# Attention and an ELU feed-forward layer on one core: the ELU's sum left in PSUM, a planner that knows a shared port, and a fourth batch taken in front

## The chip, the core and the metric

The kernel runs on one core of one Trainium2 chip. A core has TensorE (PE in the profile: matrix products, from SBUF into PSUM), VectorE (DVE) and ScalarE (ACT), which read and write SBUF and PSUM, GpSimd (POOL), which this kernel uses on SBUF only, and SyncE (SP), which here issues the transfers. Each engine works through its own queue in order. What counts is the device time of one execution, in microseconds. The median of the runs before the change is 1211.21 us (1208.86 to 1212.19).

## The reference

Causal attention with a decay bias over 8 batches, 8 heads, 576 tokens and a head size of 64, then a feed-forward layer from 512 to 2048 and back over all 4608 tokens, with ELU between. In short:

```python
scores = scale * q @ k.T                          # scale = 1/8
cum    = cumsum(maximum(s, 0))                    # per head, over the tokens
scores = where(causal, -1e9, scores + minimum(-(cum[:, None] - cum[None, :]), 0))
attn   = exp(scores - max(scores)); attn /= sum(attn) + 1e-9
x      = (attn @ v), heads side by side           # (4608, 512)
h      = x @ w_in
g      = where(h > 0, h, exp(minimum(h, 0)) - 1)
out    = g @ w_out
```

The two weight matrices are given in 64 bits; the kernel makes 32-bit values of them itself.

## The kernel before, in words

**Precision.** A value is often split into a rounded high part and the difference that is left, so that a product in a fast format keeps its accuracy: three products (high by high, low by high, high by low) in the place of one. `rounded` (line 347) makes a high part on Pool, ACT or DVE, `rest` (line 359) a low part on DVE or Pool, `psum_copy` (line 367) copies out of PSUM on ACT or DVE.

**Attention.** The 576 queries of a head are cut into a first half block of 64 and four blocks of 128, numbered 0 to 3. A block's scores see only the keys up to its end. The first batches (`N_CUT` of them, so far three) are worked in two pieces. In front, a `Low` unit takes a pair of heads with the half block and blocks 0 and 1 at once (`CUT` is 2), in plain 32-bit products, with transposes on TensorE and little splitting. Later, two `Unit`s, one for each head, take blocks 2 and 3 ("late"). A batch that isn't cut has for each pair of heads one unit for the half blocks and two whole units for blocks 0 to 3. The units that are not `Low` split queries and keys, write their weights as two 16-bit parts (`halved`, line 867) and have them transposed by DMA. For each block, `softmax_block` issues the score products (line 838), an operation on DVE that adds the mask and takes the extreme (841), and the exponential on ACT (846). The result goes to DRAM in `x_dram`.

**Feed-forward part.** The tokens, in the order in which the pieces come, are cut into 12 chunks of 384. A chunk (`moe_chunk`, line 1111) loads its x, splits it into xh and xl, and goes through 16 hidden blocks. `hidden(f)` puts 12 products into a PSUM bank `h` (line 1131; two banks in turn). Then come the exponential on ACT into `g` in SBUF (1139), the minimum with 1 less 1 on DVE (1140), the sum with the positive part of h on DVE (1142), the high part `gh` and the low part `gl`. `project(f)` issues 9 products into three output banks (line 1155). PE's order there is by the planner, often one hidden block and one projection in turn.

**Weights.** 16 blocks of each of the two matrices come in as 64-bit words. DVE and one other engine turn each into 32-bit values (lines 485 to 504), then they are split. All are used by the first chunk.

**The planner.** Nothing is issued when it is written down. `Plan.op` records an operation with the ways to do it, each an engine with an estimated cost, and with what it reads and writes. `Plan.issue` then takes one operation after the other: that which can start earliest by its own clock, and of equal ones that with the smaller priority number. Of the ways, it takes the one with the smallest start plus cost, where the cost on DVE is multiplied by a bias. The result is a fixed order of the instructions on each engine; on the chip, an instruction starts when its queue comes to it and the semaphores of its operands are there. The planner's own times are not enforced.

Of the kernel before, what the change touches and what calls it, by code (L numbers as in the profile page):

```python
# [9 lines left out]
F32 = mybir.dt.float32  # L10
# [5 lines left out]
ALU = mybir.AluOpType  # L16
# [22 lines left out]
NATIVE, WHOLE = 0, 0  # L39


N_CUT, CUT = 3, 2
PRIO_LOW = 10
SP_COST = 430.0

# [26 lines left out]
class Plan:  # L72
# [15 lines left out]
    }  # L88
    HOP = 150.0

    BIAS = {"DVE": 2.0}

    def __init__(self, tc):
        self.tc, self.nc = tc, tc.nc
# [54 lines left out]
        )  # L149

    def issue(self):
        engines = sorted({w[0] for o in self.ops for w in o.ways})
        free = dict.fromkeys(engines, 0.0)
        taken = dict.fromkeys(self.tags, 0)
        slots, skipped = {}, {}
# [14 lines left out]
        while pending:  # L170
# [96 lines left out]
def dve_p(n):  # L267

    return 155 + 1.04 * n


def dve_1(n):

    return 165 + 0.7 * n


def dve_2(n):

    return 150 + 1.5 * n


def pool_1(n):
# [8 lines left out]
def kernel(  # L291
# [43 lines left out]
    op = plan.op  # L335
    act, dve, pool, pe_ = nc.scalar, nc.vector, nc.gpsimd, nc.tensor
# [10 lines left out]
    def rounded(prio, n, dst, src, reads, writes, sign=1.0, only=None):  # L347

        ways = [
            ("Pool", pool_1(n),  # L350
             lambda: pool.tensor_scalar(dst(), src(), sign, 1.0, ALU.mult, ALU.mult)),  # L351
            ("ACT", act_s(n),
             lambda: act.activation(dst(), src(), AF.Copy, scale=sign)),  # L353
            ("DVE", dve_1(n),
             lambda: dve.tensor_scalar(dst(), src(), sign, None, ALU.mult)),
        ]
        op(prio, [w for w in ways if only is None or w[0] in only], reads, writes)

    def rest(prio, n, dst, src, hi, reads, writes, only=None):

        ways = [
            ("DVE", dve_2(n), lambda: dve.tensor_tensor(dst(), src(), hi(), ALU.subtract)),  # L362
            ("Pool", pool_2(n), lambda: pool.tensor_tensor(dst(), src(), hi(), ALU.subtract)),  # L363
        ]
        op(prio, [w for w in ways if only is None or w[0] in only], reads, writes)
# [31 lines left out]
    def decay_sums():  # L397
# [14 lines left out]
        op(-9, [("DVE", 1900.0, sums)], [], [(aux, 0), (aux, 1)])  # L412
        op(-5, [("DVE", 1300.0, parts)], [(aux, 0)], [(aux, 1), (aux, 2)])
# [57 lines left out]
    def load_unit(f, kind, src, parts):  # L471
# [7 lines left out]
        if wide:  # L479
# [11 lines left out]
                ("DVE", 500.0, lambda: dve.tensor_scalar(  # L491
                    raw.v[:, :, 1].bitcast(F32), raw.v[:, :, 1].bitcast(F32),
                    2.0**-112, None, ALU.mult)),
            ], [], [(raw, 1)])
            op(prio, [("DVE", 500.0, lambda: dve.tensor_scalar(
                raw.v[:, :, 0], raw.v[:, :, 0], 2.0**-29, 7.0, ALU.mult, ALU.min))],
               [], [(raw, 0)])

            def gather():
                dve.scalar_tensor_tensor(  # L500
                    raw.v[:, :, 0], raw.v[:, :, 1], 0x80000000, raw.v[:, :, 0],
                    ALU.bitwise_and, ALU.bitwise_or,
                )
                dve.scalar_tensor_tensor(
                    raw.v[:, :, 0], raw.v[:, :, 1], 3, raw.v[:, :, 0],
                    ALU.logical_shift_left, ALU.bitwise_or,
                )
# [319 lines left out]
    def softmax_block(prio, tag, native, pt, w, mask, mv, reads, operands, inv, view=lambda v: v):  # L827
# [21 lines left out]
        if last:  # L849
            def inverse():  # L850
                dve.tensor_scalar(sm.v[:, :ns], sm.v[:, :ns], EPS, 1.0 / up, ALU.add, ALU.mult)  # L851
                dve.reciprocal(sm.v[:, :ns], sm.v[:, :ns])  # L852

            op(prio, [("DVE", 350.0, inverse)], [], [sm])

    def normalize(prio, pt, w, sm, col):
        r = slice(col, col + 1)
        op(prio, [
            ("Pool", 160 + 1.04 * w, lambda: pool.tensor_scalar(
                pt.v[:, :w], pt.v[:, :w], sm.v[:, r], 1.0, ALU.mult, ALU.mult)),  # L860
            ("DVE", 220 + 0.7 * w, lambda: dve.tensor_scalar(
                pt.v[:, :w], pt.v[:, :w], sm.v[:, r], None, ALU.mult)),
            ("ACT", 295 + w / 1.2, lambda: act.activation(
                pt.v[:, :w], pt.v[:, :w], AF.Copy, scale=sm.v[:, r])),
# [2 lines left out]
    def halved(u, i, pt, sm, col):  # L867
# [20 lines left out]
        for part, n in ((whole, k * P), (rest, HB))[: 1 + (i == u.last)]:  # L888
# [1 line left out]
            op(prio, [  # L890
                ("Pool", 160 + 1.04 * n, lambda part=part: pool.tensor_scalar(  # L891
                    part(t16, 0), own(part), sm.v[:, r], 1.0, ALU.mult, ALU.mult)),
                ("DVE", 220 + 0.7 * n, lambda part=part: dve.tensor_scalar(
                    part(t16, 0), own(part), sm.v[:, r], None, ALU.mult)),
                ("ACT", 295 + n / 1.2, lambda part=part: act.activation(  # L895
                    part(t16, 0), own(part), AF.Copy, scale=sm.v[:, r])),
            ], [sm, (pt, "data"), (pt, "pad")], [(t16, high)])
            op(prio, [
                ("DVE", dve_2(n), lambda part=part: dve.scalar_tensor_tensor(  # L899
                    part(t16, 1), own(part), sm.v[:, r], part(t16, 0), ALU.mult, ALU.subtract)),  # L900
                ("Pool", pool_1(n) + pool_2(n), lambda part=part: scaled_rest(part)),
            ], [sm, (pt, "pad"), (t16, high)], [(t16, low), (pt, "data")])
# [208 lines left out]
    def moe_chunk(ch, rows, xc, after):  # L1111
# [11 lines left out]
        parts = {}  # L1123

        def hidden(f):
            hp = plan.buf(ps, [P, TMAX], F32, f"h_{ch}_{f}", tag="h", bufs=N_H)
            for c in range(NCB):
# [12 lines left out]
            op(side, [("DVE", dve_1(TC), lambda: dve.tensor_scalar(  # L1140
                g.v[:, :TC], g.v[:, :TC], 1.0, -1.0, ALU.min, ALU.add))], [], [g])
            op(side, [("DVE", dve_p(TC), lambda: dve.scalar_tensor_tensor(  # L1142
                g.v[:, :TC], hp.v[:, :TC], 0.0, g.v[:, :TC], ALU.max, ALU.add))], [hp], [g])
# [134 lines left out]
```

## Time and profile before

| | |
|---|---|
| median of the runs | 1211.21 us (1208.86 to 1212.19) |
| the profiled execution, its own time | 1205.16 us |
| its span, first to last instruction | 1203.4 us |
| mean granted clock of TensorE | 0.991 |
| busy PE / DVE / ACT / POOL | 1117.1 / 859.7 / 608.9 / 819.5 us |

PEld is the weight loads of TensorE, which overlap its products. A line such as L1142 is a line of the kernel; where a helper records an operation the line is the helper's, and the tile tells which operation it is (`gl<-g,gh` on L363 is the low part of the ELU's result, made on Pool). The granted clock is TensorE's, as a share of full speed. "A <- B" in a list of waits means that A stood idle until B was done.

### The profile page before, as it was taken

What the parts mean: (1) busy time and instruction counts of PE and PEld (TensorE: products, weight loads), DVE (VectorE), ACT (ScalarE), POOL (GpSimd) and SP (SyncE); (2) the same over time, 40 slices, a digit from 0 to 9 for tenths busy, and PEclk for the clock granted to TensorE, in tenths of its full rate; (3) what the DMA queues carried; (4) which work ended last, traced back from release to release, by engine and by line L of the source; (5) the groups of instructions that cost most, each with busy time, mean ns of one, the idle gap of its engine ahead of it and who ended that gap; (6) DMA issues with size and microseconds to landing.
All of it is one profiled execution on the core that took longest, in us unless ns stands there. A gap on an engine that the chain in (4) does not pass through costs nothing. (4 is left out here: it accounts for less than half of the span.)

```text
span 1203.4 us, 19946 instructions
## 1 busy us (share of the span) xinstructions
PE 1117.1 (93%) x5992; PEld 950.5 (79%) x5992; DVE 859.7 (71%) x1903; ACT 608.9 (51%) x1500; POOL 819.5 (68%) x996
## 2 busy tenths in 40 slices
PE   5788887999999999999999999999999999999998
PEld 4577766778787778878878888878877887899996
DVE  6879999899877778768787777777787777422221
ACT  4676445554555554655555555445554554332322
POOL 6787888787877656867787777777776776332322
PEclk9899899999999999999999999999999999999999
DMA  7766566867676476566576565575665565210000
GB/s 197 205 160 201 156 153 150 194 146 150 162 155 129 103 167 125 123 157 128 127 170 139 122 165 128 130 172 122 128 149 129 123 140 128 60 53 1 27 1 27
DMA packets 342316, 156.55 MB, mean 130 GB/s; under 512 B 267560, under 2 KB 321088, under 8 KB 342208
## 3 DMA queue, kind: packets, MB, share of 16 engines
q1 hardware_dynamic: 342208, 155.27, 55.6%
q8 instruction: 48, 0.79, 0.3%
q14 instruction: 60, 0.49, 0.1%
HBM read 79.66 MB, written 19.32 MB: 82 GB/s over the span
## 5 line engine op out<-in xcount | busy, mean ns | idle before, releaser
L1131 PE MATMUL h<-xh,wi 128*128 128x384 f32 x1536 | 446.6, 341 | 9.7 <-DVE g L1142 9.6
L1155 PE MATMUL o<-wo,gh 128*128 128x512 f32 x1152 | 363.8, 397 | 2.2 <-DVE mn L841 1.5
L1131 PEld LDWEIGHTS h<-xh,wi 128*128 128x128 f32 x1536 | 284.4, 189 | 20.4 <-DVE g L1142 11.7
L363 POOL TENSOR_TENSOR gl<-g,gh 128x384 fp32r<-128x384 f32 x157 | 169.7, 1081 | 158.2 <-ACT gh L353 134.5
L1131 PE MATMUL h<-xl,wi 128*128 128x384 f32 x768 | 260.2, 339 | 3.9 <-DVE xl L362 1.8
L1155 PE MATMUL o<-wo,gl 128*128 128x512 f32 x576 | 229.8, 399 | 6.1 <-POOL gl L363 3.9
L1155 PEld LDWEIGHTS o<-wo,gh 128*128 128x128 f32 x1152 | 207.9, 189 | 30.7 <-DVE mn L841 2.3
L1140 DVE TENSOR_SCALAR g<-g 128x384 f32<-128x384 f32 x192 | 102.5, 534 | 168.5 <-ACT g L1139 167.3
L846 ACT ACTIVATE p<-p,mn 128x192 f32<-128x192 f32 (+1 forms) x232 | 144.9, 625 | 90.7 <-DVE mn L841 87.7
L1139 ACT ACTIVATE g<-h 128x384 f32<-128x384 f32 x192 | 93.8, 489 | 170.8 <-PE h L1131 119.0
L899 DVE SCALAR_TENSOR_TENSOR p<-p,sm,p 128x512 f16<-128x512 f32 (+3 forms) x179 | 167.2, 957 | 14.3 <-POOL p L891 12.1
L1131 PEld LDWEIGHTS h<-xl,wi 128*128 128x128 f32 x768 | 145.2, 189 | 13.1 <-POOL xl L363 4.2
L1155 PEld LDWEIGHTS o<-wo,gl 128*128 128x128 f32 x576 | 108.3, 188 | 38.0 <-POOL gl L363 9.0
L353 ACT ACTIVATE gh<-g 128x384 fp32r<-128x384 f32 x149 | 77.7, 521 | 119.6 <-DVE g L1142 119.2
L841 DVE CUSTOM_DVE_ANT_0 p<-sc,maskw 128x192 f32<-128x192 f32 (+1 forms) x232 | 110.1, 483 | 33.8 <-PE sc L838 28.8
L969 PE MATMUL av<-T,vs 128*128 128x256 f16 (+5 forms) x896 | 119.0, 285 | 5.1 <-DMA T<-p 2.7
L969 PEld LDWEIGHTS <-vs 128*128 128x128 bf16 x896 | 79.8, 98 | 53.2 <-issue 17.2
L838 PE MATMUL sc<-kh,qs 128*128 128x288 f32 (+1 forms) x272 | 90.4, 336 | 24.8 <-DVE mn L841 24.5
L1142 DVE SCALAR_TENSOR_TENSOR g<-h,g 128x384 f32<-128x384 f32 x192 | 106.4, 554 | 4.2
L363 POOL TENSOR_TENSOR vs<-vs 128x320 f32<-128x320 f32 x102 | 84.1, 824 | 34.4 <-DMA vs<-in_vb_dram 16.9
L895 ACT ACTIVATE p<-p,sm 128x512 f16<-128x512 f32 (+2 forms) x141 | 80.6, 591 | 36.5 <-issue 17.0
L891 POOL TENSOR_SCALAR p<-p,sm 128x256 f16<-128x256 f32 (+3 forms) x100 | 63.9, 643 | 48.2 <-DVE sm L852 21.1
(143 smaller groups left out, 1642.5 us busy)
## 6 DMA issues: line engine op xcount, KB each, us to landing
stk<-in_kT_dram SPq DMA_DIRECT2D x64, 288.0 KB
vs<-in_vb_dram SPq DMA_DIRECT2D x64, 160.0 KB
stq<-in_qT_dram SPq DMA_DIRECT2D x40, 256.0 KB
w_i<-in_w_in_dram SPq DMA_DIRECT2D x16, 512.0 KB
w_o<-in_w_out_dram SPq DMA_DIRECT2D x16, 512.0 KB
out_dram<-ost SPq DMA_DIRECT2D x29, 256.0 KB
x_dram<-x_None SPq DMA_DIRECT2D x20, 288.0 KB
q<-qs SPq DMA_DIRECT2D x40, 128.0 KB
```

The source lines that it names most:

```text
L363: ("Pool", pool_2(n), lambda: pool.tensor_tensor(dst(), src(), hi(), ALU.subtract)),
L838: pe_.matmul(view(sc.v[:, :cw]), l, r, start=n == 0, stop=n == len(pairs) - 1)
L841: op(prio, [("DVE", 84 + dve_p(cw), lambda i=i, sc=sc: dve.tensor_tensor_reduce(pt.v[:, i * cw : (i + 1) * cw], sc.v[:, :cw], mv(i * cw, c ...
L846: op(prio, [("ACT", 480 + w / 1.2, lambda: act.activation(pt.v[:, :w], pt.v[:, :w], AF.Exp, bias=mn.v[:, n - 1 : n], scale=-1.0, accum_out ...
L895: ("ACT", 295 + n / 1.2, lambda part=part: act.activation(part(t16, 0), own(part), AF.Copy, scale=sm.v[:, r])),
L899: ("DVE", dve_2(n), lambda part=part: dve.scalar_tensor_tensor(part(t16, 1), own(part), sm.v[:, r], part(t16, 0), ALU.mult, ALU.subtract)),
L969: op(prio, [("PE", cost, lambda m=m, operands=operands, rows=rows: pe_.matmul(av.v[:rows, dst], *operands(), start=first and m == 0, stop= ...
L1131: pe_.matmul(hp.v[:, :TC], w_in_f[f].v[:, part, c * P : (c + 1) * P], xx.v[:, c, :TC], start=(c == 0 and m == 0), stop=(c == NCB - 1 and m ...
L1139: op(side, [("ACT", act_c(TC), lambda: act.activation(g.v[:, :TC], hp.v[:, :TC], AF.Exp))], [hp], [g])
L1140: op(side, [("DVE", dve_1(TC), lambda: dve.tensor_scalar(g.v[:, :TC], g.v[:, :TC], 1.0, -1.0, ALU.min, ALU.add))], [], [g])
L1142: op(side, [("DVE", dve_p(TC), lambda: dve.scalar_tensor_tensor(g.v[:, :TC], hp.v[:, :TC], 0.0, g.v[:, :TC], ALU.max, ALU.add))], [hp], [g])
L1155: pe_.matmul(acc[i].v, g.v[:, tb], w_out_f[f].v[:, part], start=(f == 0 and m == 0), stop=(f == NF - 1 and m == 2),)
```

## The change

Three things are changed together.

First, the ELU: the sum is written back into its PSUM bank `h` and no longer into `g`. Both parts of it are read from there: the high part by ACT or DVE, the low part by DVE. Pool has no share in either. The bank `h` is free again when the low part is made.

Second, the planner: operations of DVE that work on SBUF alone are a kind of their own, `DVE-SB`, on the same engine. The planner lets an operation of this kind or of Pool start no earlier than 300 ns before the end of the last one of either. The bias of DVE falls from 2.0 to 1.5, the cost estimates of operations on SBUF fall (`dve_1`, `dve_2`), and the two instructions of `gather` become two operations.

Third, `N_CUT` is 4: four batches are cut and have their first piece in front.

```diff
-N_CUT, CUT = 3, 2
+N_CUT, CUT = 4, 2
...
-    BIAS = {"DVE": 2.0}
+    BIAS = {"DVE": 1.5, "DVE-SB": 1.5}
+
+    PORT, PORT_LEAD = ("DVE-SB", "Pool"), 300.0
+    ENGINE = {"DVE-SB": "DVE"}
...
-                            (i, w, max(t, free[w[0]], self.ready(o, w[0])))
+                            (i, w, max(t, free[self.ENGINE.get(w[0], w[0])],
+                                       self.ready(o, self.ENGINE.get(w[0], w[0])),
+                                       port - self.PORT_LEAD if w[0] in self.PORT else 0.0))
...
+            if engine in self.PORT:
+                port = end
+            engine = self.ENGINE.get(engine, engine)
...
 def dve_1(n):
-    return 165 + 0.7 * n
+    return 165 + 0.5 * n
 def dve_2(n):
-    return 150 + 1.5 * n
+    return 160 + 1.06 * n
...
-            op(prio, [("DVE", 1450.0, gather)], [(raw, 1)], [(raw, 0)])
+            for word, how in ((0x80000000, ALU.bitwise_and), (3, ALU.logical_shift_left)):
+                op(prio, [("DVE-SB", 700.0, lambda word=word, how=how: dve.scalar_tensor_tensor(
+                    raw.v[:, :, 0], raw.v[:, :, 1], word, raw.v[:, :, 0], how, ALU.bitwise_or,
+                ))], [(raw, 1)], [(raw, 0)])
...
             op(side, [("DVE", dve_p(TC), lambda: dve.scalar_tensor_tensor(
-                g.v[:, :TC], hp.v[:, :TC], 0.0, g.v[:, :TC], ALU.max, ALU.add))], [hp], [g])
-            rounded(side, TC, lambda: gh.v[:, :TC], lambda: g.v[:, :TC], [g], [gh])
-            rest(side, TC, lambda: gl.v[:, :TC], lambda: g.v[:, :TC], lambda: gh.v[:, :TC].bitcast(F32), [g, gh], [gl])
+                hp.v[:, :TC], hp.v[:, :TC], 0.0, g.v[:, :TC], ALU.max, ALU.add))], [g], [hp])
+            psum_copy(side, TC, lambda: gh.v[:, :TC], lambda: hp.v[:, :TC], [hp], [gh])
+            op(side, [("DVE", dve_p(TC), lambda: dve.tensor_tensor(
+                gl.v[:, :TC], hp.v[:, :TC], gh.v[:, :TC].bitcast(F32), ALU.subtract))], [hp, gh], [gl])
```

What is left out: in the other operations of DVE on SBUF (`rounded`, `rest`, `normalize`, `halved`, `inverse`, the decay sums, the weights' scaling) only the kind, and for the weights' scaling the cost, is changed.

More of the change, by code (lines that the diff above doesn't have):

```diff
@@ L151, in issue @@
     def issue(self):
-        engines = sorted({w[0] for o in self.ops for w in o.ways})
+        engines = sorted({self.ENGINE.get(w[0], w[0]) for o in self.ops for w in o.ways})
+        port = 0.0
         free = dict.fromkeys(engines, 0.0)
@@ L353, in rounded @@
              lambda: act.activation(dst(), src(), AF.Copy, scale=sign)),
-            ("DVE", dve_1(n),
+            ("DVE-SB", dve_1(n),
              lambda: dve.tensor_scalar(dst(), src(), sign, None, ALU.mult)),
@@ L361, in rest @@
         ways = [
-            ("DVE", dve_2(n), lambda: dve.tensor_tensor(dst(), src(), hi(), ALU.subtract)),
+            ("DVE-SB", dve_2(n), lambda: dve.tensor_tensor(dst(), src(), hi(), ALU.subtract)),
             ("Pool", pool_2(n), lambda: pool.tensor_tensor(dst(), src(), hi(), ALU.subtract)),
@@ L410, in parts @@
             dve.tensor_tensor(lo.bitcast(F32R), sp, hi, ALU.subtract)
-        op(-9, [("DVE", 1900.0, sums)], [], [(aux, 0), (aux, 1)])
-        op(-5, [("DVE", 1300.0, parts)], [(aux, 0)], [(aux, 1), (aux, 2)])
+        op(-9, [("DVE-SB", 1900.0, sums)], [], [(aux, 0), (aux, 1)])
+        op(-5, [("DVE-SB", 1300.0, parts)], [(aux, 0)], [(aux, 1), (aux, 2)])
         for m in range(3):
@@ L490, in load_unit @@
                     2.0**-112, 1.0, ALU.mult, ALU.mult)),
-                ("DVE", 500.0, lambda: dve.tensor_scalar(
+                ("DVE-SB", 430.0, lambda: dve.tensor_scalar(
                     raw.v[:, :, 1].bitcast(F32), raw.v[:, :, 1].bitcast(F32),
@@ L494, in load_unit @@
             ], [], [(raw, 1)])
-            op(prio, [("DVE", 500.0, lambda: dve.tensor_scalar(
+            op(prio, [("DVE-SB", 430.0, lambda: dve.tensor_scalar(
                 raw.v[:, :, 0], raw.v[:, :, 0], 2.0**-29, 7.0, ALU.mult, ALU.min))],
                [], [(raw, 0)])
[L499 to L507, printed above, removed]
-            op(prio, [("DVE", 1450.0, gather)], [(raw, 1)], [(raw, 0)])
+            for word, how in ((0x80000000, ALU.bitwise_and), (3, ALU.logical_shift_left)):
+                op(prio, [("DVE-SB", 700.0, lambda word=word, how=how: dve.scalar_tensor_tensor(
+                    raw.v[:, :, 0], raw.v[:, :, 1], word, raw.v[:, :, 0], how, ALU.bitwise_or,
+                ))], [(raw, 1)], [(raw, 0)])
             words = (raw, 0)
@@ L852, in inverse @@
                 dve.reciprocal(sm.v[:, :ns], sm.v[:, :ns])
-            op(prio, [("DVE", 350.0, inverse)], [], [sm])
+            op(prio, [("DVE-SB", 350.0, inverse)], [], [sm])
     def normalize(prio, pt, w, sm, col):
@@ L860, in normalize @@
                 pt.v[:, :w], pt.v[:, :w], sm.v[:, r], 1.0, ALU.mult, ALU.mult)),
-            ("DVE", 220 + 0.7 * w, lambda: dve.tensor_scalar(
+            ("DVE-SB", 220 + 0.7 * w, lambda: dve.tensor_scalar(
                 pt.v[:, :w], pt.v[:, :w], sm.v[:, r], None, ALU.mult)),
@@ L892, in halved @@
                     part(t16, 0), own(part), sm.v[:, r], 1.0, ALU.mult, ALU.mult)),
-                ("DVE", 220 + 0.7 * n, lambda part=part: dve.tensor_scalar(
+                ("DVE-SB", 220 + 0.7 * n, lambda part=part: dve.tensor_scalar(
                     part(t16, 0), own(part), sm.v[:, r], None, ALU.mult)),
@@ L898, in halved @@
             op(prio, [
-                ("DVE", dve_2(n), lambda part=part: dve.scalar_tensor_tensor(
+                ("DVE-SB", dve_2(n), lambda part=part: dve.scalar_tensor_tensor(
                     part(t16, 1), own(part), sm.v[:, r], part(t16, 0), ALU.mult, ALU.subtract)),
```

2 lines of the change are left out of this document (1 added, 1 removed).

## The prediction

> **What bounds the kernel now.** I read the page's busy shares first, then busy time by stretch, then TensorE's waits.
>
> ```profile
> PE 1117.1 (93%) x5992; PEld 950.5 (79%) x5992; DVE 859.7 (71%) x1903; ACT 608.9 (51%) x1500; POOL 819.5 (68%) x996
> ```
>
> TensorE leads and is idle for 1203.4 - 1117.1 = 86.3 us. The view by stretch says where. Its columns: the stretch, its length, busy time and instructions of PE, weight loads, DVE, ACT, POOL, then granted clock, DMA share, GB/s.
>
> ```profile
> 0.00:97.00 97.00, 70.35 (x370) 57.20 (x370) 73.85 (x215) 63.18 (x208) 73.58 (x147) 0.95 0.74 194
> 97.00:210.00 113.00, 94.42 (x502) 79.92 (x502) 109.84 (x181) 57.57 (x131) 96.14 (x92) 0.97 0.60 159
> 210.00:300.00 90.00, 83.41 (x474) 70.91 (x475) 81.25 (x164) 45.23 (x99) 70.31 (x85) 0.98 0.74 161
> 300.00:600.00 300.00, 284.57 (x1559) 240.72 (x1557) 228.43 (x520) 161.67 (x394) 214.58 (x254) 1.00 0.62 138
> 600.00:1000.00 400.00, 389.67 (x2105) 329.08 (x2104) 303.88 (x698) 217.32 (x538) 298.80 (x355) 1.00 0.63 141
> 1000.00:1203.40 203.40, 194.63 (x988) 172.61 (x986) 62.46 (x130) 63.93 (x132) 66.07 (x68) 1.00 0.14 38
> ```
>
> PE is idle 26.7 us up to 97 (the front batches, before the first matmul of the feed-forward part), 18.6 us from 97 to 210, where DVE is busy 109.84 of 113 us (97%) and ACT only half, 22.0 us from 210 to 600, 10.3 us from 600 to 1000 (2.6%), 8.8 us behind. So DVE bounds the stretch 97 to 210; from 600 on it is PE, and there only less PE work helps. The waits (total us, times, longest) agree:
>
> ```profile
> PE sc L838 <- DVE mn L841: 24.5, 24, 2.3
> PE sc L838 <- DMA aux_dram<-aux: 9.9, 1, 9.9
> PE h L1131 <- DVE g L1142: 9.6, 10, 1.7
> ```
>
> The first and third are for DVE; the second is the start, which no part of this change touches.
>
> DVE's time is partly not work. These are groups from 97 to 210 (count | busy us, mean ns):
>
> ```profile
> L1140 DVE TENSOR_SCALAR g<-g 128x384 f32<-128x384 f32 x15 | 11.7, 778 | 0.0
> L500 DVE SCALAR_TENSOR_TENSOR w_i<-w_i 128x512 uint32<-128x512 uint32 x8 | 10.0, 1248 | 0.0
> L504 DVE SCALAR_TENSOR_TENSOR w_i<-w_i 128x512 uint32<-128x512 uint32 x8 | 9.3, 1166 | 0.3
> L500 DVE SCALAR_TENSOR_TENSOR w_o<-w_o 128x512 uint32<-128x512 uint32 x8 | 7.8, 973 | 0.2
> L504 DVE SCALAR_TENSOR_TENSOR w_o<-w_o 128x512 uint32<-128x512 uint32 x8 | 7.4, 929 | 0.3
> L495 DVE TENSOR_SCALAR w_o<-w_o 128x512 uint32<-128x512 uint32 x8 | 7.3, 916 | 0.0
> L495 DVE TENSOR_SCALAR w_i<-w_i 128x512 uint32<-128x512 uint32 x8 | 5.7, 718 | 0.0
> ...
> L363 POOL TENSOR_TENSOR gl<-g,gh 128x384 fp32r<-128x384 f32 x11 | 13.1, 1190 | 1.2 <-ACT gh L353 0.6 <-DVE sm L851 0.4
> ...
> L362 DVE TENSOR_TENSOR gl<-g,gh 128x384 fp32r<-128x384 f32 x4 | 3.7, 932 | 1.0 <-POOL gh L351 1.0
> ```
>
> and these the same lines over the whole run (count: minimum/median/maximum ns):
>
> ```profile
> L495 DVE TENSOR_SCALAR w_i<-w_i x16: 417/594/1076, 17.7 to 193.8; 128x512 uint32<-128x512 uint32 x16
> L500 DVE SCALAR_TENSOR_TENSOR w_i<-w_i x16: 680/920/1904, 19.1 to 196.1; 128x512 uint32<-128x512 uint32 x16
> L504 DVE SCALAR_TENSOR_TENSOR w_i<-w_i x16: 693/1091/1807, 19.9 to 197.8; 128x512 uint32<-128x512 uint32 x16
> ```
>
> ```profile
> L1140 DVE TENSOR_SCALAR g<-g x192: 329/360/2647, 105.6 to 1193.7; 128x384 f32<-128x384 f32 x192
> L1142 DVE SCALAR_TENSOR_TENSOR g<-h,g x192: 537/557/559, 107.4 to 1194.1; 128x384 f32<-128x384 f32 x192
> ...
> L353 ACT ACTIVATE gh<-g x149: 506/524/528, 108.0 to 1194.7; 128x384 fp32r<-128x384 f32 x149
> L362 DVE TENSOR_TENSOR gl<-g,gh x35: 545/990/1823, 109.1 to 1003.9; 128x384 fp32r<-128x384 f32 x35
> ```
>
> Operations on SBUF alone vary by 2.6 to 8 times; the one that reads PSUM (L1142) stays within 537 to 559 ns. Only the former stretch where Pool is busy, so I take the excess as time lost against Pool. From 97 to 210: L1140 15 x (778 - 360) = 6.3 us; L500, L504 and L495 8 x (1248 + 973 + 1166 + 929 + 916 + 718 - 2 x (680 + 693 + 417)) = 19.0 us, with the w_i minima for both tensors. Together 25 us of 110.
>
> **The change, part by part.**
>
> *The ELU in PSUM.* Each of the 192 hidden blocks now has its difference gl on DVE from PSUM. Price: not shown in the trace, since here DVE writes no PSUM and subtracts nothing there; bounds 545 ns (minimum of L362) and 990 ns (its median). I take L1142's 557: the same tile, one PSUM and one SBUF operand, steady. The sum now written to PSUM also stays at 557, bounds the same. From 97 to 210, 15 blocks: DVE +15 x 0.557 - 3.7 = +4.7 us (4.5 to 11.2), Pool -13.1 of 96.1 us. The copy gh on ACT reads PSUM instead of SBUF: I leave it at 524 ns, and ACT at half load hides it. In the chain of a block Pool's 1190 ns become 557.
>
> [...]
>
> *The planner.* Port rule, costs and biases add no instruction; they change which engine takes an operation and the order of the queues. Nothing makes the chip wait for the planner's port: the engines still overlap wherever their queues meet. The 25 us of excess can go entirely or not at all; with Pool's own time down 13.1/96.1 = 14% at least 3.4 us should go. Those are the bounds; I take half, -12.6 us, because the order and the choices are what the plan does decide. The split of L500/L504 into two operations issues the same two instructions: nothing.
>
> *The fourth batch in front.* Its four head pairs run blocks 0 and 1 as a Low unit and the rest late, instead of whole. A Low unit without a pause, from one first transpose to the next:
>
> ```profile
> 75.22 0.28 PE L649 MATMUL trl<-ident,pl 128*128 128x128 f32 x1
> ...
> 81.24 0.28 PE L649 MATMUL trl<-ident,pl 128*128 128x128 f32 x1
> ```
>
> 6.02 us. A late head (weighting, then scores):
>
> ```profile
> 245.42 1.46 PE L969 MATMUL av<-T,vs 128*128 128x256 f16 x14
> 246.72 0.45 PE L838 MATMUL sc<-kh,qs 128*128 128x448 f32 x1
> ...
> 247.21 0.29 PE L838 MATMUL sc<-kh,qs 128*128 128x288 f32 x1
> ```
>
> 1.30 + 0.49 + 2 x 0.27 (the two 288-column pairs, 0.13 to 0.14 a matmul) = 2.33 us. A whole head has these scores, two blocks more, and a longer weighting, and each pair of heads five small matmuls:
>
> ```profile
> 643.58 0.31 PE L838 MATMUL sc<-kh,qs 128*128 128x320 f32 x1
> ...
> 643.87 0.36 PE L838 MATMUL sc<-kh,qs 128*128 128x448 f32 x1
> ...
> 649.72 0.25 PE L838 MATMUL sc<-kh,qs 128*128 128x192 f32 x1
> ...
> 649.92 0.33 PE L838 MATMUL sc<-kh,qs 128*128 128x320 f32 x1
> ...
> 659.71 2.09 PE L969 MATMUL av<-T,vs 128*128 128x512 f16 x14
> 661.64 0.30 PE L838 MATMUL sc_None<-khs_None,qs_None 128*128 128x128 f32 x1
> 661.78 0.28 PE L838 MATMUL sc_None<-k2s,q2s 128*128 128x128 f32 x1
> ```
>
> 1.93 + 1.03 + 0.29 + 0.20 = 3.45 us a head, 2 x 3.45 + 5 x 0.14 = 7.60 a pair, against 6.02 + 4.66 = 10.68: the change adds 12.3 us of PE work. It moves 4 x 6.02 = 24.1 us to the front and takes 4 x (7.60 - 4.66) = 11.8 us from behind. DVE in the front:
>
> ```profile
> 0.00:97.00 97.00, 21.41 (x118) 0.95 0.74 194
> ```
>
> This is L841, two instructions a block and five blocks a unit: 118/10 = 11.8 units before 97. Less 16 weight units (half of the 32; the other 16 are the groups from 97 to 210) at 0.594 + 0.920 + 1.091 = 2.6 us, DVE's 73.85 us leave 32 us, 2.7 us a unit; four add 10.9 us (bounds 4 x 1.8 from L841 alone and 4 x 6.3 from all of it). Their loads and stores pass SP's queue in front:
>
> ```profile
> kl<-in_kT_dram SPq DMA_DIRECT2D x12, 160.0 KB
> ```
>
> Queries and result are as large and the values 224 KB by the code: 0.7 MB a unit, 14.5 us in all at the front's 194 GB/s, beside a DMA share of 0.60 to 0.74: hidden. If that cover were gone, the price is 14.5 us.
>
> *The sum.* Stretch 97 to 210: DVE 109.8 + 4.7 - 12.6 + 10.9 = 112.8 us, at 97% busy 116 us. PE 94.4 + 24.1 = 118.5 us, at the 97.4% of the stretch from 600 to 1000, 121.7 us. PE is late next: +8.7 us. Batch 3's smaller rest: 11.8/0.974 = -12.1 us. From 210 to 600 PE is idle 5.6%; down to 2.6% would be -12 us, and with half of the excess gone I take half, -6. From 600 to 1000: -2, of 10.3 us idle. Before 97 and behind 1000: nothing. Sum -11.4 us: the span becomes 1192.0. The profiled execution's own time is 1205.16 us, 1.8 above its span, and the median of the runs is 1211.21, 6.05 above that; I add the difference to the median: 1199.8, say **1200 us**.
>
> **Rivals.**
>
> *The four Low units are not filled* (slower). Before 97 a unit takes (97 - 9.9)/11.8 = 7.4 us, not 6.02, because PE waits for scores, normalisation and copies. If the feed-forward part does not enter between the added ones, the front grows by 4 x 7.4 = 29.6 us: +29.6 - 12.1 - 6 - 2 = +9.5, 1221 us. It decides once the first feed-forward matmul moves from 97 to about 127. For it: units have their priority ahead. Against it: feed-forward matmuls already run among the last units at 97.
>
> *The plan's port is only a plan.* Only 3.4 us of excess go: DVE 109.8 + 4.7 - 3.4 + 10.9 = 122 us, stretch 125.5 us, +12.5; -12.1; nothing else: 1211.6 us. For it: no wait enforces it. The change then doesn't do what it says.
>
> *The bank is held longer.* h is freed after gl, not after the sum: 0.524 + 0.557 us and two hand-overs, about 1.35 us. If the 10 waits of PE for g grow by this, +13.5: -11.4 + 13.5, 1213 us; behind such a wait PE's whole queue stands. Against it: with two banks and 5.7 us a block (1100 us over 192), the slack is several us from 300 on.
>
> *The port is the bound.* If DVE on SBUF and Pool exclude each other, all the excess can go: also before 97, where 16 weight units at median less minimum, 16 x 0.815 = 13 us of DVE, give PE two thirds, 8.5 us; PE's idle share from 210 to 600 falls to 2.6% (-12), 600 to 1000 gives half its idle time (-5): +8.7 - 12.1 - 8.5 - 12 - 5 = -28.9, 1182 us. For it: maxima of 1904 and 2647 ns, a whole Pool instruction and more. [...]
>
> **How the numbers follow.** Forecast 0.38 (1200), port 0.20 (1182), unfilled front 0.21 (1221), plan only 0.13 (1212), bank 0.08 (1213). The measurement tells about 0.3%, 3.6 us, from no change: below 1207.6 is faster. Faster: 0.20, most of the forecast (0.35), and a share of the two middle ones (0.05): 0.60. The same: 0.14, mostly the middle ones. Slower: 0.26. The range, 1179 to 1224, takes in the port case and the unfilled front; DVE's dearer bounds (gl at 990, units at 6.3 us) give +6.5 and +14.3 us in the first stretch and stay within it. The forecast's own: 1191 to 1209.
>
> **What would show it.** Right: no gl on Pool, gl on DVE near 557 ns; L1140 and L500 to L504 nearer their minima from 97 to 210; PE there above 95% busy; 12 us more PE work at the same clock; PE idle below 75 us in all. Wrong: DVE on SBUF as slow as before; the first feed-forward matmul 20 us or more later with PE as idle as now ahead of it; waits of PE for gl's release of h.

## The result, and the profile after

The changed kernel takes 1151.99 us (median, 1149.54 to 1154.58), the kernel before in the same comparison 1210.25. The ratio is 0.952, with a 95% interval of 0.949 to 0.954: 58 us less, where the prediction had 11. The time lies outside its range, 1179 to 1224. (The 1211.21 us given above as the median before is one of these four runs; half-way between the middle two is 1210.25.)

The profiled execution took 1151.57 us, with this span and these busy times:

```profile
span 1149.7 us, 19957 instructions
PE 1105.7 (96%) x6080; PEld 961.7 (84%) x6080; DVE 868.8 (76%) x2161; ACT 564.9 (49%) x1412; POOL 517.6 (45%) x766
```

DVE makes all 192 low parts of the ELU, 157 more than before, yet its busy time is nearly the same (868.8 for 859.7 us). Pool's falls by 302 us, of which its 157 low parts of the ELU were 170. The view by stretch, with the columns of before:

```profile
0.00:97.00 97.00, 79.02 (x440) 65.03 (x441) 81.00 (x255) 67.66 (x227) 68.89 (x150) 0.98 0.76 202
97.00:210.00 113.00, 104.59 (x589) 91.30 (x588) 105.66 (x233) 67.06 (x163) 71.53 (x93) 1.00 0.67 175
210.00:300.00 90.00, 87.65 (x520) 77.72 (x520) 74.79 (x185) 43.51 (x98) 50.76 (x72) 1.00 0.77 159
300.00:600.00 300.00, 295.06 (x1676) 256.79 (x1675) 248.58 (x626) 154.10 (x370) 149.64 (x209) 1.00 0.70 153
600.00:1000.00 400.00, 394.88 (x2142) 341.22 (x2142) 301.73 (x757) 194.65 (x478) 169.22 (x235) 1.00 0.55 127
1000.00:1149.70 149.70, 144.50 (x721) 129.63 (x719) 57.04 (x109) 37.94 (x77) 7.54 (x10) 1.00 0.07 22
```

TensorE's idle time (length less PE busy) by stretch:

| us | before | after |
|---|---|---|
| 0 to 97 | 26.7 | 18.0 |
| 97 to 210 | 18.6 | 8.4 |
| 210 to 300 | 6.6 | 2.3 |
| 300 to 600 | 15.4 | 4.9 |
| 600 to 1000 | 10.3 | 5.1 |
| 1000 to the end | 8.8 | 5.2 |
| all | 86.3 | 44.0 |

So 42 us of the 53.7 by which the span is shorter are pauses gone, in every stretch. The granted clock has risen too. One less the clock, times the PE time of each stretch, is 0.05 x 70.35 + 0.03 x 94.42 + 0.02 x 83.41 = 8.0 us before and 0.02 x 79.02 = 1.6 us after: 6 us. Against this stand the 12.3 us of work that the fourth batch adds. The remaining 17 us or so are busy time in which products follow each other more densely; no view divides it. The waits of TensorE:

```profile
PE sc L840 <- POOL k L432: 9.4, 1, 9.4
PE h L1133 <- DVE gl L1148: 4.8, 7, 1.5
PE sc L840 <- DVE mn L843: 4.4, 9, 0.7
```

The first is the start, as before. The wait of score products for the mask operation (line 843, formerly 841), 24.5 us before, is 4.4. The bank h, now held until gl is made, costs 4.8 us over 7 waits, where the shorter hold cost 9.6 over 10. The groups on DVE from 97 to 210:

```profile
L509 DVE SCALAR_TENSOR_TENSOR w_o<-w_o 128x512 uint32<-128x512 uint32 x18 | 14.0, 778 | 0.2
L509 DVE SCALAR_TENSOR_TENSOR w_i<-w_i 128x512 uint32<-128x512 uint32 x16 | 13.2, 826 | 0.7 <-ACT w_i L494 0.7
L1142 DVE TENSOR_SCALAR g<-g 128x384 f32<-128x384 f32 x17 | 10.2, 602 | 1.9 <-ACT g L1141 1.8
...
L1148 DVE TENSOR_TENSOR gl<-h,gh 128x384 fp32r<-128x384 f32 x17 | 9.3, 548 | 0.3 <-ACT gh L378 0.3
```

They are shorter than before (L509 holds both former lines, 929 to 1248 ns; L1142 is the former L1140, 778 ns). That looks like the prediction's account, in which the excess on DVE, its time above the shortest durations, goes. The experiments show that it isn't what carries the gain.

### The profile page after: what moved, and what is told of

It reads as the page before. It is cut to its first block, busy times and chain, and to the rows that moved or that the text cites. A ratio compares the mean times of both kernels' runs of the same rounds, so it can differ in the third digit from the quotient of the medians.

```text
span 1149.7 us, 19957 instructions
## 1 busy us (share of the span) xinstructions
PE 1105.7 (96%) x6080; PEld 961.7 (84%) x6080; DVE 868.8 (76%) x2161; ACT 564.9 (49%) x1412; POOL 517.6 (45%) x766
## 4 chain that ended last, share of the span: by engine, by line
PE 73%; DVE 12%; DMA 5%; issue 3%; POOL 3%; ACT 2%; SPq 1%; POOLq 0%; DVEq 0%; ACTq 0%
PE o L1159 28%; PE h L1133 28%; PE sc L840 8%; PE av L971 7%; DVE p L901 2%; DVE g L1142 1%; DVE p L843 1%; DMA T<-p 1%; DMA stq<-in_qT_dram 1%; PE avl L646 1%; DVE h L1145 1%; DVE xl L371 1%; SPq L348 1%; DVE gl L1148 1%; PE trl L665 1%
## 5 line engine op out<-in xcount | busy, mean ns | idle before, releaser
L1142 DVE TENSOR_SCALAR g<-g 128x384 f32<-128x384 f32 x192 | 87.9, 458 | 110.6 <-ACT g L1141 109.5
L901 DVE SCALAR_TENSOR_TENSOR p<-p,sm,p 128x512 f16<-128x512 f32 (+3 forms) x207 | 158.2, 787 | 6.8 <-ACT p L897 3.3
L378 ACT CAST gh<-h 128x384 fp32r<-128x384 f32 x179 | 85.6, 478 | 142.5 <-DVE h L1145 135.2
L1148 DVE TENSOR_TENSOR gl<-h,gh 128x384 fp32r<-128x384 f32 x192 | 106.1, 552 | 44.5 <-ACT gh L378 41.8
L893 POOL TENSOR_SCALAR p<-p,sm 128x512 f16<-128x512 f32 (+2 forms) x135 | 91.6, 686 | 104.6 <-DVE sm L854 34.5
L372 POOL TENSOR_TENSOR vs<-vs 128x320 f32<-128x320 f32 x85 | 69.7, 820 | 106.5 <-DMA vs<-in_vb_dram 59.3
L971 PE MATMUL av<-T,vs 128*128 128x256 f16 (+5 forms) x896 | 114.1, 279 | 3.3 <-DMA T<-p 2.1
L1145 DVE SCALAR_TENSOR_TENSOR h<-h,g 128x384 f32<-128x384 f32 x192 | 107.8, 561 | 3.7
L840 PE MATMUL sc<-kh,qs 128*128 128x288 f32 (+1 forms) x256 | 83.2, 329 | 4.5 <-DVE mn L843 4.4
L840 PE MATMUL sc<-k,q 128*128 128x288 f32 (+1 forms) x256 | 79.1, 314 | 2.2 <-POOL k L372 2.0
```

The costliest lines, as they stand in the source:

```text
L840: pe_.matmul(view(sc.v[:, :cw]), l, r, start=n == 0, stop=n == len(pairs) - 1)
L901: ("DVE-SB", dve_2(n), lambda part=part: dve.scalar_tensor_tensor(part(t16, 1), own(part), sm.v[:, r], part(t16, 0), ALU.mult, ALU.subtract)),
L971: op(prio, [("PE", cost, lambda m=m, operands=operands, rows=rows: pe_.matmul(av.v[:rows, dst], *operands(), start=first and m == 0, stop= ...
L1142: op(side, [("DVE-SB", dve_1(TC), lambda: dve.tensor_scalar(g.v[:, :TC], g.v[:, :TC], 1.0, -1.0, ALU.min, ALU.add))], [], [g])
L1148: op(side, [("DVE", dve_p(TC), lambda: dve.tensor_tensor(gl.v[:, :TC], hp.v[:, :TC], gh.v[:, :TC].bitcast(F32), ALU.subtract))], [hp, gh], ...
```

## The experiments

Medians with the ratio to the kernel before, measured in the same comparison, and its 95% interval. The theories' names are those of the expectations.

### Each part alone, and in pairs

The ELU's edit alone, on the kernel before:

```diff
             op(side, [("DVE", dve_p(TC), lambda: dve.scalar_tensor_tensor(
-                g.v[:, :TC], hp.v[:, :TC], 0.0, g.v[:, :TC], ALU.max, ALU.add))], [hp], [g])
-            rounded(side, TC, lambda: gh.v[:, :TC], lambda: g.v[:, :TC], [g], [gh])
-            rest(side, TC, lambda: gl.v[:, :TC], lambda: g.v[:, :TC], lambda: gh.v[:, :TC].bitcast(F32), [g, gh], [gl])
+                hp.v[:, :TC], hp.v[:, :TC], 0.0, g.v[:, :TC], ALU.max, ALU.add))], [g], [hp])
+            psum_copy(side, TC, lambda: gh.v[:, :TC], lambda: hp.v[:, :TC], [hp], [gh])
+            op(side, [("DVE", dve_p(TC), lambda: dve.tensor_tensor(
+                gl.v[:, :TC], hp.v[:, :TC], gh.v[:, :TC].bitcast(F32), ALU.subtract))], [hp, gh], [gl])
```

> The kernel before with the ELU's edit alone: the sum in its PSUM bank, high part from there on ACT or DVE, low part from there on DVE; planner and three batches as before. Theory port (the gain is that DVE's SBUF operations and Pool's no longer stand in each other's way): Pool loses 160 to 190 us of work, the excess of L1140 and of the weights' groups on DVE falls by a fifth or so, 1185 to 1200 us. Theory front (the fourth batch carries the gain): 1200 to 1212. Theory chain (the ELU's chain of a hidden block, 0.6 us shorter without Pool, is the gain): 1160 to 1175, with most of the 42 us less idle TensorE here already.

Measured 1200.98 us, 0.991 (0.988 to 0.993): 11 us, just above the range of "port" and inside that of "front". "Chain" is out.

The planner's edits alone, that is, the changed kernel with the ELU and the number of batches as before:

```diff
-N_CUT, CUT = 4, 2
+N_CUT, CUT = 3, 2
...
-                hp.v[:, :TC], hp.v[:, :TC], 0.0, g.v[:, :TC], ALU.max, ALU.add))], [g], [hp])
+                g.v[:, :TC], hp.v[:, :TC], 0.0, g.v[:, :TC], ALU.max, ALU.add))], [hp], [g])
...
```

> The kernel before with the planner's edits alone (port rule, costs, bias, the split gather); ELU through SBUF and three batches as before. Theory port: DVE's SBUF operations near their minima, 1175 to 1190 us. Theory front: 1200 to 1212. Theory chain: 1200 to 1215, since gl stays on Pool or on SBUF.

Measured 1179.34 us, 0.974 (0.971 to 0.976): 33 us, the largest single part, as "port" had it in time. Its durations are not near their minima, though: the operation on g takes 451 ns on the mean, at a minimum of 340.

The fourth batch alone, on the kernel before:

```diff
-N_CUT, CUT = 3, 2
+N_CUT, CUT = 4, 2
```

> The kernel before with four batches cut instead of three, nothing else. Theory port: no gain, since 12 us more TensorE work meet a front that is still held by DVE: 1208 to 1222 us. Theory front: 1165 to 1190. Theory chain: as port, 1208 to 1222.

Measured 1211.88 us, 1.0005 (0.999 to 1.002): nothing. "Front" is out as a cause by itself.

The changed kernel with three batches:

```diff
-N_CUT, CUT = 4, 2
+N_CUT, CUT = 3, 2
```

> The changed kernel with three batches cut instead of four. Theory port: nearly all of the gain, 1150 to 1165 us, and the fourth batch is worth at most 10 us either way. Theory front: 1180 to 1200. Theory chain: 1155 to 1170.

Measured 1177.43 us, 0.972 (0.969 to 0.975): only 35 us, a miss for "port". The fourth batch, worth nothing on the kernel before, is worth 25 us on top of the other two. So the parts don't add up, and the remaining pairs were run, with theories of their own.

The changed kernel with the first diff of this section turned round (plan_four), and the kernel before with that diff and a fourth batch (elu_four):

> The changed kernel with the ELU's edit undone (sum in SBUF, gl on DVE or Pool), planner and fourth batch kept. Theory pair (the planner makes DVE quick enough, the fourth batch then fills the stretch from 160 to 240 us where TensorE still ran dry and lost its clock): 1150 to 1162 us, less than 4 us lost at a lowered clock, the ELU's edit worth 10 us at most. Theory ELU (the fourth batch pays only with the ELU's edit): 1172 to 1182 us, as the planner alone.

> The kernel before with the ELU's edit and the fourth batch, planner as before. Theory pair: DVE still collides with Pool, so the fourth batch adds little to the ELU's 11 us: 1192 to 1204 us. Theory ELU: 1165 to 1185 us.

Measured 1156.81 us, 0.955 (0.953 to 0.958), and 1199.72 us, 0.990 (0.987 to 0.993). Both as "pair" had it: planner and fourth batch give 55 of the 58 us between them. The ELU's edit adds some 4 us on top, barely told from nothing: the intervals of the two ratios, 0.953 to 0.958 and 0.949 to 0.954, overlap.

Where the fourth batch's 25 us lie is seen in the kernel with three (elu_plan), by stretch:

```profile
97.00:210.00 113.00, 97.20 (x484) 79.35 (x483) 104.84 (x215) 58.73 (x123) 73.61 (x80) 0.89 0.70 177
210.00:300.00 90.00, 86.64 (x503) 76.40 (x502) 74.05 (x183) 47.43 (x105) 47.26 (x63) 0.96 0.73 162
```

Its clock is 0.89 and 0.96 here, in the changed kernel 1.00. In the middle of it, in steps of 5 us:

```profile
160.00:165.00 5.00, 2.84 (x14) 2.03 (x12) 4.36 (x13) 1.81 (x4) 4.25 (x7) 0.98 1.04 211
165.00:170.00 5.00, 4.16 (x18) 2.97 (x18) 4.90 (x10) 3.68 (x7) 2.29 (x2) 0.50 0.65 167
170.00:175.00 5.00, 5.00 (x22) 4.27 (x22) 5.00 (x11) 1.75 (x5) 3.81 (x5) 0.84 0.83 181
175.00:180.00 5.00, 2.08 (x9) 1.12 (x9) 4.96 (x10) 2.38 (x6) 2.33 (x3) 0.85 1.12 272
180.00:185.00 5.00, 5.00 (x20) 3.90 (x18) 4.90 (x7) 2.38 (x4) 4.59 (x5) 0.50 0.29 105
```

PE stands for 2.2 us from 160 to 165 and for 2.9 us from 175 to 180, and each time the next 5 us run at half the clock. Over all stretches this kernel loses 15.7 us to the clock, the changed one 1.6; its idle time is 1180.0 - 1114.6 = 65.4 us, the changed one's 44.0. That is 14 + 21 = 35 us, less 12 us for the added work: 23 of the 30 us by which the two profiled executions differ (their spans are 1180.0 and 1149.7 us; the medians are 25 apart). The fourth batch pays by being there when PE would stand; with the 21 us of pauses went 14 us lost to the clock. The waits of PE that the view of this kernel lists from 150 to 225 are 11, 16.6 us together, the longest 3.0 us.

### What in the planner

The port rule off, the new cost estimates and biases kept:

```diff
-    PORT, PORT_LEAD = ("DVE-SB", "Pool"), 300.0
+    PORT, PORT_LEAD = (), 300.0
```

> The changed kernel with the planner's port rule switched off (Pool and DVE on SBUF planned side by side), cost estimates and biases as changed. Theory port rule: the planner again puts Pool beside DVE, Pool's busy time back to 600 us or more, DVE's SBUF operations stretched: 1185 to 1205 us. Theory estimates (the lower costs and bias, which move work from Pool to DVE, are what counts): 1150 to 1162 us.

Measured 1199.85 us, 0.990 (0.988 to 0.993): 48 us of the gain are lost with one line. This is also the time of the ELU's edit and the fourth batch with the old planner (1199.72): the new estimates and biases are worth nothing without the rule. DVE's operations are stretched, as "port rule" expected (the operation on g takes 520 ns on the mean, 458 in the changed kernel). But Pool's busy time did not go back to 600 us; it is 554:

```profile
PE 1124.1 (94%) x6080; PEld 965.4 (80%) x6080; DVE 909.7 (76%) x2149; ACT 562.7 (47%) x1409; POOL 554.4 (46%) x794
```

So most of the work taken from Pool isn't the rule's doing. The estimates and bias as before, port rule kept:

```diff
-    BIAS = {"DVE": 1.5, "DVE-SB": 1.5}
+    BIAS = {"DVE": 2.0, "DVE-SB": 2.0}
...
-    return 165 + 0.5 * n
+    return 165 + 0.7 * n
...
-    return 160 + 1.06 * n
+    return 150 + 1.5 * n
```

> The changed kernel with the two cost functions and the bias of DVE as before (0.7 and 1.5 ns an element, bias 2.0), port rule kept. Theory port rule: 1152 to 1168 us, work kept apart though DVE is thought slow. Theory estimates: 1180 to 1205 us, with Pool's busy time at 600 us or more.

Measured 1169.98 us, 0.966 (0.964 to 0.969), a little above what "port rule" had. With the rule, then, the new estimates are worth 18 us. One of the groups on DVE (busy us, mean ns of one | idle time before, and what ended it), first of the kernel before, then of this one:

```profile
L1140 DVE TENSOR_SCALAR g<-g 128x384 f32<-128x384 f32 x192 | 102.5, 534 | 168.5 <-ACT g L1139 167.3
```

```profile
L1142 DVE TENSOR_SCALAR g<-g 128x384 f32<-128x384 f32 x192 | 113.0, 588 | 155.8 <-ACT g L1141 154.5
```

This operation is stretched no less than before, and yet the kernel is 42 us faster than the one before, and 30 us faster than the ELU's edit and the fourth batch with the old planner. For this group, then, the prediction's account does not hold. Taken over all of DVE's operations the excess did fall. As an estimate from the traces, take each operation less the shortest one of the same tiles and shape in any run: that gives 254 us before, 160 here and 127 in the changed kernel. So this run alone does not settle it; the next ones do.

The rule can act in two ways: through the engine that it chooses for an operation, and through the order of the queues. To part them, the planner ran twice, the first time only to fix the engines. (The second pass also deals out the buffers anew, so their placement counts as order here.)

```diff
+        self.PORT = self.PORT_CHOICE
+        self.run(picks)
...
+            o.ways = [o.ways[picks[o]]]
...
+        self.PORT = self.PORT_ORDER
+        return self.run(None)
```

> The planner runs twice: a first pass, with the port rule, only fixes which engine takes each operation; a second pass, with the port rule and these engines, writes the order. A control for the next two: some orders differ from the changed kernel's, engines don't. Every theory: 1148 to 1162 us.

> Engines as the port rule chooses them, order of the queues planned without the rule. Theory choice (the rule's gain is that less is given to Pool and DVE at once): as the control, 1150 to 1165 us. Theory order (the gain is an order that fits the pace at which DVE and Pool really deliver, so that TensorE's queue seldom stands at a product whose operand is late): 1185 to 1205 us, with TensorE's waits for L843 and for gl of 30 us and more.

> Engines as they are chosen without the rule, order planned with the rule. Theory choice: 1185 to 1205 us. Theory order: 1150 to 1170 us.

Measured: with the rule in both passes 1152.91 us, 0.953 (0.949 to 0.956); in the choice alone 1196.40, 0.988 (0.985 to 0.992); in the order alone 1176.80, 0.971 (0.969 to 0.974). The choice alone gives 3 us over no rule at all (1199.85), which the intervals do not tell from nothing, the order alone 23 us, a little short of what "order" had, and both 47: engines and order have to belong together, but without the order there is next to nothing.

The first two of these kernels run the same instructions on the same engines, 43 us apart. Their pages:

```profile
PE 1106.3 (96%) x6080; PEld 963.4 (84%) x6080; DVE 869.4 (76%) x2161; ACT 560.9 (49%) x1412; POOL 509.3 (44%) x766
```

```profile
PE 1122.5 (94%) x6080; PEld 967.6 (81%) x6080; DVE 890.3 (75%) x2161; ACT 563.2 (47%) x1412; POOL 522.9 (44%) x766
```

Two groups on DVE, first with the rule in both passes, then in the choice alone:

```profile
L921 DVE SCALAR_TENSOR_TENSOR p<-p,sm,p 128x512 f16<-128x512 f32 x122 | 104.1, 863 | 4.3 <-POOL p L913 2.3 <-ACT p L917 1.3
L1162 DVE TENSOR_SCALAR g<-g 128x384 f32<-128x384 f32 x192 | 90.7, 473 | 101.8 <-ACT g L1161 100.1
```

```profile
L921 DVE SCALAR_TENSOR_TENSOR p<-p,sm,p 128x512 f16<-128x512 f32 x122 | 109.9, 917 | 12.5 <-POOL p L913 7.6 <-ACT p L917 4.3
...
L1162 DVE TENSOR_SCALAR g<-g 128x384 f32<-128x384 f32 x192 | 92.7, 483 | 112.2 <-ACT g L1161 111.7
```

The durations differ by 2 to 6%, DVE's whole busy time by 21 of 890 us, and DVE is busy three quarters of the time in both. The largest difference is in TensorE's waiting. The spans are 1150.3 and 1195.0 us, so PE is idle for 44.0 and 72.5 us: 28 of the 45 us. The other 16 are busy time of PE, for the same products; some 6 of them are the lower clock (4.4 us lost to it with the rule in both passes, 10.2 in the choice alone, counted in steps of 5 us), and the rest is not explained. Its largest waits from 300 to 1000, first with the rule in both passes:

```profile
PE h L1153 <- DVE gl L1168: 4.7, 6, 1.2
...
PE sc L860 <- DVE mn L863: 0.5, 1, 0.5
```

```profile
PE h L1153 <- DVE gl L1168: 11.9, 10, 2.5
PE sc L860 <- DVE mn L863: 6.8, 7, 2.1
```

They are waits at the head of PE's queue for a result that comes later than its place in the queue. Over the whole run these two waits come to 5.5 and 0.5 us with the rule in both passes, and in the choice alone to 29 us, where "order" had 30 and more:

```profile
PE h L1153 <- DVE gl L1168: 18.2, 15, 2.5
PE sc L860 <- DVE mn L863: 10.7, 10, 2.1
```

Is that because any plan with late results will do? The rule off, and every operation of Pool and of DVE on SBUF counted 1.4 times as long:

```diff
-    PORT, PORT_LEAD = ("DVE-SB", "Pool"), 300.0
+    PORT, PORT_LEAD, SLOW = (), 300.0, 1.4
...
-            end = start + cost
+            end = start + cost * (self.SLOW if engine in ("DVE-SB", "Pool") else 1.0)
```

> The changed kernel without the port rule, but the planner counts every operation of Pool and of DVE on SBUF 1.4 times as long. Theory pace (any plan that expects late results is as good as the rule): 1150 to 1170 us. Theory exclusion (the plan has to know which operation stands in the way of which): 1180 to 1205 us.

Measured 1173.27 us, 0.968 (0.965 to 0.972), short of "pace" and better than "exclusion" had it: 27 us over no rule, somewhat over half of the rule's 48. A slower pace in the plan is part of it. That the rest comes from knowing which operations exclude each other is not shown: here the engines of some operations changed too. Both are theories of how the order becomes better; only that it is the order is shown.

### Place of the sum, figure of the rule, one batch more

The sum left in SBUF, but its high part on ACT only and its low part on DVE only:

```diff
-                hp.v[:, :TC], hp.v[:, :TC], 0.0, g.v[:, :TC], ALU.max, ALU.add))], [g], [hp])
+                g.v[:, :TC], hp.v[:, :TC], 0.0, g.v[:, :TC], ALU.max, ALU.add))], [hp], [g])
-            psum_copy(side, TC, lambda: gh.v[:, :TC], lambda: hp.v[:, :TC], [hp], [gh])
-            op(side, [("DVE", dve_p(TC), lambda: dve.tensor_tensor(
-                gl.v[:, :TC], hp.v[:, :TC], gh.v[:, :TC].bitcast(F32), ALU.subtract))], [hp, gh], [gl])
+            rounded(side, TC, lambda: gh.v[:, :TC], lambda: g.v[:, :TC], [g], [gh], only=("ACT",))
+            rest(side, TC, lambda: gl.v[:, :TC], lambda: g.v[:, :TC], lambda: gh.v[:, :TC].bitcast(F32), [g, gh], [gl], only=("DVE-SB",))
```

> The changed kernel with the ELU's sum in SBUF as before, but the high part on ACT only and the low part on DVE only. Tells the place of the sum apart from the engine of gl. Theory engine (only that gl has left Pool counts): 1148 to 1156 us, as the changed kernel, gl near 600 ns. Theory place (PSUM keeps gl out of Pool's way): 1158 to 1172 us, gl at 650 ns or more.

Measured 1151.84 us, 0.953 (0.951 to 0.955): the time of the changed kernel. The low part costs more there, and is hidden:

```profile
L371 DVE TENSOR_TENSOR gl<-g,gh 128x384 fp32r<-128x384 f32 x192 | 125.1, 652 | 41.9 <-ACT gh L362 23.0 <-PE o L1157 17.8
```

So the sum's place in PSUM has no part in the time that can be measured; "engine" had the time right, "place" the duration of gl.

A stricter and a looser rule, with 0 and with 600 ns; the first is

```diff
-    PORT, PORT_LEAD = ("DVE-SB", "Pool"), 300.0
+    PORT, PORT_LEAD = ("DVE-SB", "Pool"), 0.0
```

> The changed kernel with the port's lead at 0 instead of 300 ns, a stricter rule. Theory order: the rule's presence counts, not its exact figure, 1148 to 1165 us. If the rule's gain were from collisions avoided on the chip, a stricter one would collide less: 1140 to 1150 us.

> The changed kernel with the port's lead at 600 ns, a looser rule: operations of up to 600 ns are no longer kept apart. Theory order: 1150 to 1175 us, part of the way to the 1200 us without the rule.

Measured 1154.37 us, 0.955 (0.953 to 0.957), and 1185.32 us, 0.981 (0.979 to 0.983). With a lead of 0 DVE's operation on g is near its median of 360 ns on the mean:

```profile
L1142 DVE TENSOR_SCALAR g<-g 128x384 f32<-128x384 f32 x192 | 75.6, 394 | 127.0 <-ACT g L1141 125.6
```

394 ns for the changed kernel's 87.9 us over 192, 458 ns: 12 us less on DVE for this group, and no time gained. With 600 ns some 70% of the rule's worth (33 of 48 us) is gone, more than expected, at much the same durations (477 ns).

The count of the excess over all of DVE's operations says the same. It is 87 us with a lead of 0, for 1154 us, and 127 in the changed kernel, for 1152. And at nearly the same excess, 148 to 162 us, the kernels take anything from 1152 to 1196 us: 162 with the sum in SBUF (1151.84), 160 with the old estimates (1169.98), 154 with the slower pace (1173.27), 150 with a lead of 600 ns (1185.32), 148 with the rule in the choice alone (1196.40). So the lost time on DVE does not decide the time of the kernel.

That the durations go with Pool's work is seen in the trace of the kernel before: the 75 operations on g beside which no instruction of Pool ran took 340 to 362 ns, the other 117 from 329 to 2647. In that of the changed kernel gl from PSUM took 538 to 559 ns in 92 such cases and 525 to 559 in the other 100. The 394 ns of the operation on g with a lead of 0, and the 520 in the kernel without the rule, agree with this; but here the time does not follow the durations. By what the two engines hold each other up, no run shows.

Five batches cut:

```diff
-N_CUT, CUT = 4, 2
+N_CUT, CUT = 5, 2
```

> The changed kernel with five batches cut. Each adds about 12 us of TensorE work, and behind 97 us TensorE is idle for 25 us at most in the changed kernel. Theory filling (the fourth paid because it filled pauses and kept the clock up): nothing is left to fill, 1155 to 1168 us. Theory front (cut batches are cheaper as such): 1135 to 1148 us.

Measured 1171.39 us, 0.969 (0.966 to 0.971): 19 us slower than with four. PE's busy time is 1119.4 us, 14 more, and its idle time 50.8 us, 7 more. "Filling" had the sign and nearly the size. The worth of cutting a batch is the pauses that it fills, less its work: 0 on the kernel before, 25 us for the fourth on the new planner, -19 for the fifth. None of these kernels is faster than the changed one by more than the measurement tells.

## Why the prediction was wrong, point by point

**What bounds the kernel: right in part.** TensorE bounds it and pauses were to be gained; but all of them, not only those of the stretch where DVE was at 97%. The prediction took 97.4% busy, the share from 600 to 1000, as TensorE's ceiling. After the change it is 98.4% from 300 to 600 and 98.7% from 600 to 1000.

**"I take half, -12.6 us": the step that failed.** The planner was costed as DVE time saved from Pool. DVE's operations did become shorter (the groups from 97 to 210 above), but this isn't what the planner is worth: at nearly the same excess on DVE kernels took from 1152 to 1196 us, and with operations within 2 to 6% of the control's only 3 us came from the choice of engines. In its place the runs show the order of the queues, worth 23 us by itself and 47 with the engines that belong to it. The step fed the sum's -6 and -2 us behind 210 as well: from 210 to 1000 not 8 us of pauses went but 20.

**"The plan's port is only a plan": the rival with the wrong reason.** It is true that no wait enforces the port, and the kernel without the rule is 48 us slower all the same. An order that is written by a planner *is* the planner's effect: where the head of PE's queue was a product whose operand was late, PE stood (18.2 us for the bank h in the choice alone, 5.5 in the control). The prediction looked for the planner's worth in the durations that it might shorten and gave the order no term.

**"Before 97: nothing": wrong.** 8.7 us of pauses went there too, with 440 PE instructions where there were 370. The planner's edits alone do this; by the views of those kernels PE's idle time before 97 is 19.0 us with them and 25.5 with the fourth batch alone.

**The fourth batch: alone right, together wrong.** +8.7 and -12.1 made it worth 3 us; alone it measured 0. Its TensorE work was put at +12.3 us; PE's busy time rose by 9.5 us alone (1126.6 for 1117.1). What the sum lacked is the time lost to the clock, which was 0.89 from 97 to 210 in the kernel with three batches (0.11 x 97.20 = 10.7 us), and that it is the planner that makes the front able to take the work.

**The unfilled front: seen, in the other kernels.** This rival's mark was a first feed-forward product about 30 us later. The first exponential of a hidden block starts at 103.3 us before and at 101.7 in the changed kernel, but at 131.0 in the kernel with the fourth batch alone and at 129.5 in the one with the rule in the choice alone. It is not the order by itself that fills the front. With the rule in the order alone the first exponential starts later still, and that kernel is 20 us faster than the one with the rule in the choice alone:

```profile
L1161 ACT ACTIVATE g<-h x192: 467/492/512, 134.4 to 1165.3; 128x384 f32<-128x384 f32 x192
```

With a lead of 600 ns, or with the slower pace in place of the rule, it starts at 128.5 and 132.1; only where the rule of at most 300 ns stood in both choice and order did it start at about 111 us or before, with four batches. The rival's price of 1221 us was too high: alone it came to 1211.9.

**The ELU's pieces: right in size.** gl was put at 557 ns on DVE and takes 548 to 556, the sum written to PSUM 561 on the mean, and the copy gh on ACT 480 for the assumed 524. On the new planner gl on DVE takes 652 ns from SBUF, from PSUM 552, on the mean. But that does not count: the kernel with the sum in SBUF loses nothing by it (1151.84 us). The bank, held longer, is not a wait that grew in the changed kernel (4.8 us for 9.6 before); in the choice alone, with the same hold, it is 18.2.

**The range.** The port rival (1182 us) was the most that was thought possible, and it was bounded by the DVE time of the front. That DVE on SBUF and Pool exclude each other was its premise; no run shows more of this than the durations beside Pool (329 to 2647 ns for the operation on g in the kernel before). Taken stretch by stretch, the idle time of 86.3 us, the lowered clock (8 us) and busy time in which products follow each other less densely were all open to a better order; the range should have reached to them.

**What stays open.** About 17 us of the span are denser busy time that no view divides. Why one order is better is known only in part: a slower pace in the plan gives about half of it. And why the new estimates are worth 18 us with the rule and nothing without it was not looked into.

## What to carry to other kernels

Where a planner or a hand fixes the order of the queues, its model of time is part of the kernel: here two orders of the same instructions on the same engines were 43 us apart, with DVE's durations within a few per cent and its share of busy time the same. Look for it in the waits at the head of the busiest engine's queue, and test it by holding engines fixed and changing only the order. Work that fills pauses is worth what it fills, so such edits have to be judged together: here cutting one batch more was worth 0, 25 and -19 us.

## What the runs showed of the hardware that was not expected

Pauses of TensorE went together with a lower clock behind them: in steps of 5 us, in the kernel with three batches, the granted clock was 0.50 behind stretches in which PE had stood for 2.2 and 2.9 of 5 us, though no single wait there was over 3.0 us. With PE busy for 4.16 and 5.00 us of the steps behind them, that is 2.1 and 2.5 us lost to the clock. Summed over such steps, the time lost to the clock was 1.4 us in the changed kernel and 17.7 in the one with the planner's edits alone, as much as many an edit is worth.

A difference of a PSUM and an SBUF operand on DVE kept within 525 to 559 ns over the 192 instructions of the changed kernel, where the same difference with both operands in SBUF, in the kernel with the sum left there, went from 527 to 3043 ns, with a median of 559: half of them took no longer than that, and the mean of 652 hides it.
